# Block 1 of a fused chunk-attention and bilinear-FFN kernel laid out by hand, with the out stores joined in pairs and moved to ScalarE's queue

## The chip, the cores and the metric

The kernel runs on one core of one Trainium2 chip. The metric is the device time of one execution in microseconds (us); below, a time is the median over several executions, with their range. Most executions of one kernel agree within about 1.5%; those more than 1.5% above the fastest of their kernel are labelled slow, and no ratio uses them.

Engine names are those of the profile: PE is TensorE, PEld its weight loads, DVE is VectorE, ACT is ScalarE, POOL is GpSimd, SP is SyncE, and SPq and ACTq are the DMA-issuing instructions of SP and ACT.

## The reference

Attention in chunks of 64 tokens, then a feed-forward layer that multiplies two projections. Inputs and output are fp32.

```python
# q, k, v: (8 batches, 8 heads, 576, 64), cut along the sequence into chunks of 64
scores = (q_c @ k_c^T) / sqrt(64)              # 64x64 in each chunk and head
attn   = exp(scores - max) / (sum + 1e-9)
x      = (attn @ v_c) -> (4608 tokens, 512)    # heads side by side
out    = ((x @ w_a) * (x @ w_b)) @ w_out       # w_a, w_b: 512x1536, w_out: 1536x512
```

## The kernel before

The 4,608 tokens are handled as nine blocks of 512 tokens (K = 0 to 8); a block is two units of 256 (U = 0 to 17). For each unit q, k and v are loaded, cast to bf16 by GpSimd, and q and k are transposed: on TensorE for units 0 to 5, by DMA from unit 6 on (`bring`). The feed-forward layer has six column pairs per block. Block 0 computes them plainly (`ab_step`). From block 1 on, a pair can be done with seven products in place of eight (a Winograd-like scheme, `Group` with `p1` to `p7`), which needs sums of the weights (`combine_w`, four VectorE instructions per pair) and of x. Block 1 does its first two pairs plainly (`PLAIN = 2`). The third product of the kernel, `out_part`, is cut into three parts for each of the four tiles of a block; the third part copies the result to an `o_sb` buffer and stores it.

```python
PE_UNITS = 6
PLAIN = 2
...
    b_pool = ctx.enter_context(tc.tile_pool(name="bsb", bufs=2))
    c_pool = ctx.enter_context(tc.tile_pool(name="csb", bufs=2))
    o_pool = ctx.enter_context(tc.tile_pool(name="osb", bufs=3))
...
    def transpose_dma(U):
        for w, n in ((0, "q"), (1, "k")):
            nc.sync.dma_start_transpose(out=..., in_=raw.pop((n, U))...)   # cut

    def bring(U):
        cast(U, "qk")
        load(U + 1, "q")
        if U < NU:
            transpose_dma(U)
        cast(U, "v")
        load(U + 1, "kv")
...
    def out_part(K, tg, part):
        if part == 0:
            out_ps[K, tg] = bank(psum)
        for ft in range(4 * part, 4 * part + 4):
            nc.tensor.matmul(...)                                           # cut
        if part == 2:
            u, c = divmod(tg, 2)
            o_sb = o_pool.tile([128, DM], FP32, name="o_sb")
            nc.vector.tensor_copy(out=o_sb, in_=out_ps.pop((K, tg)))
            for g in range(2):
                r0 = K * BLK + 256 * u + 128 * g + 64 * c
                nc.sync.dma_start(out=out[r0:r0 + 64, :], in_=o_sb[g * 64:g * 64 + 64, :])
...
        for ft in range(NFT):                     # block 0
            ab_step(0, ft)
            if ft % 2:
                combine_w(ft // 2)
            ...
        cast(4); cast(5); load(6)
        for U in range(PE_UNITS, 8):
            bring(U)
        ...
        for ft in range(2 * PLAIN):               # block 1, the plain pairs
            ab_step(1, ft, 0, 256)
            ...
```

The softmax here doesn't subtract the row's maximum and nothing guards it: scores larger than these inputs give would overflow.

## Time and profile before

| what | value |
|---|---|
| time, 4 executions beside the changed kernel | 332.56 us (330.32 to 334.37) |
| start of block 1, from TensorE's timeline | 47.1 us |
| start of block 2 (first product of its first pair) | 94.5 us |
| from there to the end | 235.6 us, 31.3 us per block on average |
| out stores | 70 on SP's queue, 128 KB each, 2.4 us from issue to landing |

First, the page's slices: the span in 40 equal parts, busy tenths of TensorE, its granted clock in tenths, and the mean busy share of the 16 DMA engines.

```profile
PE   2979784899789999999999999999999999999995
...
PEclk9999799999959999999999999999999999999999
DMA  8999999999989999876978596964111111111223
```

TensorE is full, and at full clock, from the thirteenth slice on. Before that, the DMA engines are full and TensorE and its clock have holes. From slice 29 on (231 us), the loads are over and DMA falls to one tenth: the store traffic that remains is small.

Next, the timeline of TensorE: start, length, line, operation, and in brackets the idle time before it and what ended that.

```profile
51.48 0.60 PE L329 MATMUL ps<-xT,wa 128*128 128x256 f16 x4 [2.05 <-DVE ab_sb L338]
...
58.60 0.61 PE L329 MATMUL ps<-xT,wb 128*128 128x256 f16 x4 [2.80 <-DVE xT L285]
...
92.23 0.63 PE L228 MATMUL ps<-qkt 64*64 64x64 bf16 x30 [3.33 <-DVE o_sb L448]
```

Three holes in block 1: an accumulator bank not yet free, x of unit 3 not yet ready, and an `o_sb` buffer not yet stored. The stage table shows what the last one costs. Its columns are start:end, length, busy us (and instructions) of PE, PEld, DVE, ACT and POOL, granted clock, DMA share, GB/s.

```profile
88.90:92.20 3.30, 0.00 (x0) 0.00 (x0) 0.72 (x2) 0.00 (x0) 1.86 (x2) 0.80 1.02 269
92.20:97.70 5.50, 5.47 (x54) 3.48 (x54) 4.59 (x9) 2.87 (x6) 0.00 (x0) 0.50 0.70 159
97.70:129.00 31.30, 30.43 (x374) 21.37 (x372) 20.10 (x34) 21.28 (x38) 9.37 (x9) 1.00 1.05 218
```

After the hole of 3.3 us TensorE runs 5.5 us at half clock. From 97.7 us on it is full at full clock. In block 2, the DMA engines have no time to spare.

Why the buffer came late is seen in the waits of VectorE (total us, count, longest) and in the timeline of SP's queue (start, length, DMA, count):

```profile
DVE o_sb L448 <- DMA out_dram<-o_sb: 4.0, 1, 4.0
```

```profile
78.13 1.75 SPq L156 DMA_DIRECT2D st<-in_q_dram  x2
80.05 2.84 SPq L210 DMA_TRANSPOSE qkt<-q_raw  x1
82.99 1.25 SPq L210 DMA_TRANSPOSE qkt<-k_raw  x1
...
87.66 5.64 SPq L451 DMA_DIRECT2D out_dram<-o_sb  x8
```

The stores of block 0 are issued at 87.66 us, behind the loads and transposes of units 7 and 8, which stand on the same queue.

### The profile page before, as it was taken

To read this page: it belongs to the slowest core of one execution; us is meant where nothing else is said; L and a number is where in the kernel's file an instruction comes from. 1 tells how busy PE (TensorE), PEld (TensorE's weight loads), DVE (VectorE), ACT (ScalarE), POOL (GpSimd) and SP (SyncE) were. 2 spreads that over 40 slices of the span, in tenths; PEclk is the share of its full clock that TensorE was granted. 3 is DMA by queue.
4 is the path that set the end of the run, shared out by engine and by line. 5 is a ranking of instruction groups with operands and counts; after the bars stand their busy time and mean duration, and the time that the engine had idled before them with its cause. 6 is when DMAs were issued, how large, how long until landed. Compare 5 with 4: busy or idle time off the path is not lost.

```text
span 330.1 us, 7886 instructions
## 1 busy us (share of the span) xinstructions
PE 303.6 (92%) x3222; PEld 205.7 (62%) x3222; DVE 216.7 (66%) x350; ACT 172.2 (52%) x307; POOL 74.6 (23%) x76
## 2 busy tenths in 40 slices
PE   2979784899789999999999999999999999999995
PEld 1534353766556667676777666777776677777743
DVE  3459895746365678587758766857595768666551
ACT  1733355375457655656566566565656464444400
POOL 1566665633213322222121212120000000000000
PEclk9999799999959999999999999999999999999999
DMA  8999999999989999876978596964111111111223
GB/s 238 328 374 284 274 367 230 258 218 246 224 186 236 219 168 233 201 159 162 145 178 179 141 158 163 187 155 110 32 30 38 32 34 34 32 35 43 52 65 96
DMA packets 139331, 53.98 MB, mean 164 GB/s; under 512 B 114592, under 2 KB 133280, under 8 KB 139296
## 3 DMA queue, kind: packets, MB, share of 16 engines
q1 hardware_dynamic: 139136, 53.36, 69.6%
q8 instruction: 25, 0.41, 0.5%
q10 hardware_dynamic: 160, 0.13, 0.2%
q14 instruction: 10, 0.08, 0.1%
HBM read 37.75 MB, written 9.44 MB: 143 GB/s over the span
## 4 chain that ended last, share of the span: by engine, by line
PE 65%; DMA 17%; SPq 8%; DVE 5%; POOL 2%; issue 1%; ACT 1%; ACTq 0%; POOLq 0%; DVEq 0%
PE ps L438 21%; PE pb L375 17%; PE pc L375 11%; PE ps L375 10%; DMA st<-in_moe_w_a_dram 7%; DMA st<-in_q_dram 5%; SPq L156 5%; DMA st<-in_v_dram 4%; PE ps L460 3%; PE ps L243 1%; DVE s L355 1%; SPq L168 1%; SPq L210 1%; PE ps L228 1%; PE ps L276 1%
## 5 line engine op out<-in xcount | busy, mean ns | idle before, releaser
L438 PE MATMUL ps<-wo,ab_sb 128*128 128x512 bf16 x384 | 97.9, 379 | 0.0
L375 PEld LDWEIGHTS <-t 128*128 128x128 f16 x736 | 69.2, 98 | 18.2 <-issue 4.8
L413 DVE TENSOR_TENSOR c_sb<-pc,v_sb 128x512 f32<-128x512 f32 x46 | 31.8, 691 | 55.2 <-ACT v_sb L386 55.2
L375 PE MATMUL pb<-s,t 128*128 128x256 f16 x368 | 56.4, 277 | 0.5 <-ACT u_sb L386 0.5
L375 PE MATMUL ps<-xT,wb 128*128 128x256 f16 x368 | 55.7, 274 | 0.0
L386 ACT COPY u_sb<-pb 128x512 f32<-128x512 f32 x46 | 27.0, 586 | 52.1 <-PE pb L375 52.1
L438 PEld LDWEIGHTS <-ab_sb 128*128 128x128 bf16 x384 | 37.6, 98 | 25.7
L425 DVE TENSOR_TENSOR ab_sb<-pc,c_sb 128x512 bf16<-128x512 f32 x46 | 31.7, 689 | 12.2 <-PE pc L375 11.7
L375 PEld LDWEIGHTS <-wb 128*128 128x128 f16 x368 | 36.3, 99 | 4.5
L425 DVE TENSOR_TENSOR ab_sb<-pb,b_sb 128x512 bf16<-128x512 f32 x46 | 31.5, 685 | 4.4 <-PE pb L375 4.4
L386 ACT COPY v_sb<-pb 128x512 f32<-128x512 f32 x46 | 27.1, 589 | 13.1 <-PE pb L375 12.2
L183 POOL CAST q_raw<-st 128x1024 bf16<-128x1024 f32 x17 | 17.7, 1040 | 71.2 <-DMA st<-in_q_dram 65.6
L414 DVE TENSOR_TENSOR pc<-pc,u_sb 128x512 f32<-128x512 f32 x46 | 31.7, 690 | 0.0
L393 ACT COPY pb<-ps 128x512 f32<-128x512 f32 x46 | 27.3, 594 | 7.7 <-PE ps L375 7.7
L236 ACT ACTIVATE E<-ps 128x512 bf16<-128x512 f32 x34 | 18.6, 594 | 21.8 <-PE ps L228 21.8
L375 PE MATMUL pc<-xT,t 128*128 128x256 f16 x184 | 27.6, 272 | 0.6 <-DVE pc L414 0.5
L375 PE MATMUL pb<-s,wa 128*128 128x256 f16 x184 | 28.1, 276 | 0.0
L375 PE MATMUL pc<-s,t 128*128 128x256 f16 x184 | 28.1, 276 | 0.0
L448 DVE COPY o_sb<-ps 128x512 f32<-128x512 f32 x32 | 21.9, 685 | 9.1 <-PE ps L438 5.0
L183 POOL CAST k_raw<-st 128x1024 bf16<-128x1024 f32 x17 | 17.7, 1040 | 43.8 <-DMA st<-in_k_dram 42.9
L386 ACT COPY b_sb<-ps 128x512 f32<-128x512 f32 x46 | 27.3, 594 | 0.0
L253 ACT ACTIVATE ln<-ps 128x512 f32<-128x512 f32 x34 | 18.6, 595 | 15.6 <-PE ps L243 15.6
(67 smaller groups left out, 312.8 us busy)
## 6 DMA issues: line engine op xcount, KB each, us to landing
out_dram<-o_sb SPq DMA_DIRECT2D x70, 128.0 KB, 2.4
st<-in_v_dram SPq DMA_DIRECT2D x32, 256.0 KB, 4.2
st<-in_q_dram SPq DMA_DIRECT2D x23, 256.0 KB, 4.3
st<-in_k_dram SPq DMA_DIRECT2D x23, 256.0 KB, 3.6
st<-in_moe_w_b_dram SPq DMA_DIRECT2D x6, 512.0 KB, 7.0
st<-in_moe_w_a_dram SPq DMA_DIRECT2D x6, 512.0 KB, 8.0
st<-in_moe_w_out_dram SPq DMA_DIRECT2D x6, 512.0 KB, 7.1
st<-in_q_dram SPq DMA_DIRECT2D x4, 512.0 KB, 5.4
```

The costliest lines, as they stand in the source:

```text
L156: nc.sync.dma_start(out=st[p:p + n, g], in_=src[b, :, s:s + n, :].rearrange("h p d -> p h d"))
L183: eng.tensor_copy(out=raw[n, U], in_=staged.pop((n, U)))
L236: nc.scalar.activation(out=E_of[U][:, j], in_=sc[j], func=AF.Exp, scale=scale)
L253: nc.scalar.activation(out=ln_of[U][:, cl].rearrange("p m n -> p (m n)"), in_=sm[cl], func=AF.Ln)
L375: nc.tensor.matmul(t[:, h * 256:h * 256 + 256], w[:, kt, h * 128:h * 128 + 128], x[:, kt], start=start and h == 0 and kt == 0, stop=h == 1 ...
L386: nc.scalar.copy(out=t, in_=src)
L393: nc.scalar.copy(out=self.B, in_=self.A)
L413: nc.vector.tensor_tensor(out=self.c, in0=self.C, in1=self.v, op=ADD)
L414: nc.vector.tensor_tensor(out=self.C, in0=self.C, in1=self.u, op=ADD)
L425: nc.vector.tensor_tensor(out=self.dst[:, :, c0:c0 + 256], in0=t.rearrange("p (h n) -> p h n", h=2), in1=o.rearrange("p (h n) -> p h n", h=2),
L438: nc.tensor.matmul(out_ps[K, tg], ab_tiles[K][:, ft, tg * 128:tg * 128 + 128], w_out[ft], start=(ft == 0), stop=(ft == NFT - 1),)
L448: nc.vector.tensor_copy(out=o_sb, in_=out_ps.pop((K, tg)))
```

## The change

The intent was to fill the holes of block 1: two more plain pairs, so that weight sums can leave block 0 and be spread in pairs over block 1; unit 3 started first; more buffers for `b_sb`; and the out stores taken off SP's queue, so that they no longer wait behind loads. The core of the diff:

```diff
-PLAIN = 2
+PLAIN = 4
...
-    def combine_w(i):
+    def combine_w(i, part):                      # two of the four sums at a time
...
+            ("wa", (psum_c, psum)[ft % 2] if whole else psum_c),
...
-        b_sb = b_pool.tile([128, BLK], FP32, name="b_sb")
+        b_sb = c_pool.tile([128, BLK], FP32, name=("b_sb", "u_sb", "v_sb", "c_sb")[ft % 4])
...
-            for g in range(2):
-                r0 = K * BLK + 256 * u + 128 * g + 64 * c
-                nc.sync.dma_start(out=out[r0:r0 + 64, :], in_=o_sb[g * 64:g * 64 + 64, :])
+            stores.append((K * BLK + 256 * u, c, o_sb))
+
+    stores = []
+
+    def store():
+        while stores:
+            r0, c, o_sb = stores.pop(0)
+            nc.scalar.dma_start(
+                out=out[r0:r0 + 256, :].rearrange("(g c r) d -> c g r d", g=2, c=2)[c],
+                in_=o_sb,
+            )
...
         for ft in range(NFT):
             ab_step(0, ft)
-            if ft % 2:
-                combine_w(ft // 2)
+            if ft in (9, 10):
+                combo()                          # one half of combine_w
...
         def chunk():
+            store()
             if outs:
                 out_part(*outs.pop(0))
...
+        transpose_pe(3)
         for ft in range(2 * PLAIN):
             ab_step(1, ft, 0, 256)
...
+            if ft >= 5:                          # out parts of block 0 start here
+                chunk()
+                combo()
+        transpose_pe(4)
...                                              # attention of units 4 to 6 re-placed
```

Before, a tile went out as two stores of 64 rows each; now as one store whose DRAM side is 2 x 64 rows of 512.

More of the change, by code (lines that the diff above doesn't have):

```diff
@@ L59 @@
     ab_pool = ctx.enter_context(tc.tile_pool(name="ab", bufs=2))
-    b_pool = ctx.enter_context(tc.tile_pool(name="bsb", bufs=2))
     c_pool = ctx.enter_context(tc.tile_pool(name="csb", bufs=2))
@@ L109 @@
     w_t = {}
-    def combine_w(i):
+    def combine_w(i, part):
         wb, wa = w_ab["wb", i], w_ab["wa", i]
         b11, b12, b21, b22 = wb[:, 0:2], wa[:, 0:2], wb[:, 2:4], wa[:, 2:4]
-        t1, t2, t3, t4 = [
-            wpool.tile([128, 2, WCOL], FP16, name=f"t{j}_{i}") for j in range(1, 5)
-        ]
+        if i not in w_t:
+            w_t[i] = [wpool.tile([128, 2, WCOL], FP16, name=f"t{j}_{i}") for j in range(1, 5)]
+        t1, t2, t3, t4 = w_t[i]
         for o, x0, x1, op in (
-            (t1, b12, b11, SUB),
-            (t3, b22, b12, SUB),
-            (t2, t3, b11, ADD),
-            (t4, b21, t2, SUB),
-        ):
+            ((t1, b12, b11, SUB), (t3, b22, b12, SUB)),
+            ((t2, t3, b11, ADD), (t4, b21, t2, SUB)),
+        )[part]:
             nc.vector.tensor_tensor(out=o, in0=x0, in1=x1, op=op)
-        w_t[i] = (t1, t2, t3, t4)
     def load_wo(i):
@@ L134, in cast_wo @@
         t = wpool.tile([128, 2, DM], BF16, name=f"wo{i}")
-        nc.gpsimd.tensor_copy(out=t, in_=staged.pop(("wo", i)))
+        src = staged.pop(("wo", i))
         for f in range(2):
+            nc.gpsimd.tensor_copy(out=t[:, f], in_=src[:, f])
             w_out[2 * i + f] = t[:, f, :]
@@ L325, in ab_step @@
         ps = {}
-        for n, pool in (("wb", psum_b), ("wa", psum_c)):
-            ps[n] = bank(pool if c1 - c0 == BLK else psum)[:, :c1 - c0]
+        whole = c1 - c0 == BLK
+        for n, pool in (
+            ("wb", psum_b if whole else psum),
+            ("wa", (psum_c, psum)[ft % 2] if whole else psum_c),
+        ):
+            ps[n] = bank(pool)[:, :c1 - c0]
             for kt in range(NKT):
@@ L382, in product, with staged @@
                     )
-        def staged(self, src, name, pool):
-            t = pool.tile([128, 512], FP32, name=name)
+        def staged(self, src, name):
+            t = c_pool.tile([128, 512], FP32, name=name)
             nc.scalar.copy(out=t, in_=src)
@@ L396, in p6 @@
             self.product(self.B, self.t2, self.s2)
-            self.u = self.staged(self.B, "u_sb", c_pool)
+            self.u = self.staged(self.B, "u_sb")
         def p2(self):
             self.product(self.A, self.b21, self.x12)
-            self.b = self.staged(self.A, "b_sb", b_pool)
+            self.b = self.staged(self.A, "b_sb")
         def p5(self):
             self.product(self.B, self.t1, self.s1)
-            self.v = self.staged(self.B, "v_sb", c_pool)
+            self.v = self.staged(self.B, "v_sb")
         def p7(self):
@@ L532, with combo @@
         spread[:] = [psum]
+        combos = [(i, p) for i in range(PLAIN, NWP) for p in range(2)]
+        combos += [(i, p) for i in range(PLAIN) for p in range(2)]
+        def combo():
+            if combos:
+                combine_w(*combos.pop(0))
         for ft in range(NFT):
             ab_step(0, ft)
-            if ft % 2:
-                combine_w(ft // 2)
+            if ft in (9, 10):
+                combo()
             if ft == 6:
@@ L559, in values_x @@
                 combine_x(U // 2)
+        transpose_pe(3)
         for ft in range(2 * PLAIN):
             ab_step(1, ft, 0, 256)
-            if ft == 0:
-                transpose_pe(3)
-            if ft == 2:
+            if ft == 1:
                 scores(3)
-        sums(3)
-        inverse(3)
-        values_x(3)
+                combo()
+            if ft == 3:
+                sums(3)
+                inverse(3)
+        values(3)
+        outs += [(0, tg, p) for tg in range(4) for p in range(3)]
         for ft in range(2 * PLAIN):
             ab_step(1, ft, 256, 512)
-        attention = {
-            (1, PLAIN, 0): [lambda: transpose_pe(4)],
-            (1, PLAIN, 1): [lambda: scores(4)],
-            (1, PLAIN + 1, 0): [lambda: sums(4), lambda: inverse(4), lambda: transpose_pe(5)],
-            (1, PLAIN + 1, 1): [lambda: scores(5)],
-            (1, PLAIN + 2, 0): [lambda: values_x(4)],
-            (1, PLAIN + 2, 1): [lambda: sums(5)],
-            (1, PLAIN + 3, 0): [lambda: inverse(5)],
-            (1, PLAIN + 3, 1): [lambda: values_x(5), lambda: scores(6)],
+            if ft in (1, 2):
+                combo()
+            if ft == 3:
+                combine_x(1)
+            if ft >= 5:
+                chunk()
+                combo()
+        transpose_pe(4)
+        attention = {
+            (1, PLAIN, 0): [chunk, lambda: scores(4)],
+            (1, PLAIN, 1): [chunk, combo, lambda: transpose_pe(5), combo],
+            (1, PLAIN + 1, 0): [lambda: sums(4), lambda: inverse(4), combo],
+            (1, PLAIN + 1, 1): [lambda: scores(5), chunk, lambda: values_x(4)],
             (2, 0, 0): [lambda: sums(6), lambda: inverse(6)],
@@ L614 @@
             for i in range(PLAIN if K == 1 else 0, NWP):
-                if (K, i) in ((1, PLAIN), ) or (K > 1 and i == 1):
+                if K > 1 and i == 1:
                     outs += [(K - 1, tg, p) for tg in range(4) for p in range(3)]
@@ L634 @@
                 chunk()
-                if K == 1:
-                    chunk()
                 attend(K, i, 1)
@@ L640 @@
                 last = now
+            if K == 1:
+                sums(5)
+                inverse(5)
+                chunk()
+                combo()
+                chunk()
+                values_x(5)
+                while outs:
+                    chunk()
+                combo()
+                scores(6)
+                store()
+                assert not combos
         last.add7()
@@ L647 @@
             chunk()
+        store()
         for tg in range(4):
```

## The prediction

> **What bounds the kernel now.** The granted clock is full and TensorE is about 100% busy from 98 us on (slices, stage table), so blocks 2 to 8 run at TensorE's pace and the change can move little there. The loss is before: between the start of block 1 (47.1 us) and the first product of block 2 (94.5 us) the timeline of TensorE shows idle gaps of 2.05, 2.80 and 3.33 us and smaller ones, and after the last of them 5.5 us at a granted clock of 0.50, about 11 us in all. Block 0 loses about 4.7 us more (a 2.1 us wait for a VectorE copy queued behind the weight sums, then half clock). Through 90 us the 16 DMA engines are full (share 1.0 to 1.1). The chain that ended last runs through loads, casts and DMA issues up to 88.5 us, then an out store, then TensorE. The 3.33 us gap is an o_sb buffer waiting for its store (4.0 us), which stood on the SP queue behind the loads of units 7 and 8.
>
> **What the change removes.** 20 of 24 weight sums (0.41 us alone, up to 1.26 us) leave block 0: I estimate block 0 ends 4 us earlier. Two more plain pairs cost 8 matmuls of 0.109 us, 0.9 us. Deeper b_sb and alternating banks remove most gaps of 2 to 3 us in the plain half. If nothing else happened, block 2 would start near 84 us, 10 us earlier.
>
> **What it adds.** Each out store is now an instruction of ScalarE, which stops there until the store's semaphores are reached. The built program shows more than the diff: eight DMA semaphores are handed out in turn, and each DMA waits for the one before it on its semaphore. The first store (block 0, tile 0) waits for unit 7's DMA transpose of q, the second for that of k, the third for the load of v of unit 8. In the trace unit 7's transposes are issued at 80.05 and 82.99 us and land 4.9 and 2.9 us later; they hang on loads, casts and the earlier transposes, none of which the change speeds up. ScalarE reaches the first store near 64 us. So I expect it to stand there until about 85 us. TensorE can go on only until the next out part needs a bank that an E activation of unit 4 has to free, so it idles some 17 to 20 us.
>
> **What remains after 85 us**, by durations in the trace: about 16 us of TensorE work up to the fourth product of block 2, which the kernel before issues at 99.7 us. Add 1.2 us (store, first activation), 2.5 us for 5 us at half clock (the Trainium skill, "TensorE: Matmul & The Clock Gate", What's actually happening, says the clock halves after an idle window of about 3.4 us; this trace agrees: 3.33 us idle, then 5.5 us at 0.50), and 2 to 3 us because ScalarE has to catch up. That gives 106 to 107 us: 6 to 7 us later. The gains of block 0 vanish in the wait. From block 2 on I expect no change; a store costs ScalarE 0.5 to 0.7 us, 4 per 31 us, off the path.
>
> **Prediction:** 340.0 us, 80% range 331.0 to 345.0. Faster by over 2%: 0.10; within 2%: 0.42; slower by over 2%: 0.48.
>
> **What shows it.** Right: ScalarE idle some 20 us before the first E of unit 4, ended by a DMA; TensorE idle there, slices near 0 between 67 and 85 us, half clock after. Wrong: stores issued near 65 us, block 2 starting before 90 us.
>
> **What would make it wrong.** Transposes landing much earlier; a store's wait not holding ScalarE; the 2% line lies at 339.9 us, so a microsecond decides the class.

## More of the kernel before

Finally, the DMA queues, with packets, MB and share of the 16 engines' time:

```profile
q1 hardware_dynamic: 139136, 53.36, 69.6%
...
q10 hardware_dynamic: 160, 0.13, 0.2%
```

q1 is SP's queue, q10 ScalarE's. ScalarE issues only two stores of the last tile here.

## The result, and the profile after

The changed kernel takes **381.27 us** (375.67 to 382.51, four executions) against 332.56 us (330.32 to 334.37) of the kernel before on the same chip. The ratio is 1.138, with a 95% interval of 1.119 to 1.157. It is 13.8% slower, and outside the predicted range of 331 to 345 us. (Each ratio in this document is the mean time of one kernel's fast runs over that of the other's of the same rounds, so not quite the ratio of the medians quoted.) The output is correct.

The profiled execution took 381.4 us.

The page's slices after; a slice is 9.5 us here, 8.25 us before:

```profile
PE   2799877608888792967929778999999999999994
...
PEclk9999999957989997896978969999999999999999
DMA  8999999995799699967899899983110111111114
```

There is one deep hole in slices 8 and 9, as predicted. But TensorE and its clock also show losses in slices 14 to 25, where the kernel before was full. The DMA engines are no less busy there (0.90 to 1.05 of their time from 140 to 233 us, against 0.75 to 0.86 from 129 to 222 us before), yet they move no more: 139 to 164 GB/s against 166 to 168.

**The hole in block 1.** ScalarE's timeline and TensorE's after it:

```profile
69.30 0.65 ACT L394 COPY pb<-ps 128x512 f32<-128x512 f32 x1
84.46 1.16 ACTq L457 DMA_DIRECT2D out_dram<-o_sb  x1
85.66 0.60 ACT L233 ACTIVATE E<-ps 128x512 bf16<-128x512 f32 x1 [15.71 <-issue]
```

```profile
86.31 1.86 PE L439 MATMUL ps<-wo,ab_sb 128*128 128x512 bf16 x4 [13.54 <-ACT E L233]
```

ScalarE ended a copy at 69.9 us, issued its first out store at 84.46 us, and came to E of unit 4 at 85.66 us. (E is the program's tile of exp(scores); it is not the theory E below.) TensorE stood 13.5 us for it. Block 2 starts at 101.7 us, 7.2 us later than before. This is close to what was predicted (about 85 us, and 6 to 7 us later).

**The loss after that.** From the start of block 2 to the end the kernel takes 277.8 us, against 235.6 before: 42.2 us more, where no change was predicted. TensorE's timeline has a hole like these in several blocks:

```profile
149.90 1.01 PE L376 MATMUL pb<-s,wa 128*128 128x256 f16 x4 [7.49 <-ACT v_sb L387]
...
173.21 1.01 PE L376 MATMUL pb<-s,wa 128*128 128x256 f16 x4 [5.51 <-ACT v_sb L387]
...
198.32 1.01 PE L376 MATMUL pb<-s,wa 128*128 128x256 f16 x4 [7.02 <-ACT v_sb L387]
```

TensorE waits for ScalarE's copy `v_sb`. What did ScalarE wait for? Its waits (total, count, longest):

```profile
ACT ln L259 <- DMA st<-in_v_dram: 16.8, 2, 8.7
...
ACT ln L259 <- DMA qkt<-q_raw: 6.7, 1, 6.7
...
ACT E L233 <- DMA qkt<-k_raw: 5.2, 1, 5.2
```

No ln and no E reads these DMAs' data: `ln` at L259 reads the ln tile itself, and E the bank of scores. The store just ahead of them in ScalarE's order is what waits, and the profile counts its wait to the next computing instruction. ScalarE's timeline before the first of TensorE's holes above shows it, down to the copy that TensorE waits for:

```profile
147.75 0.52 ACTq L457 DMA_DIRECT2D out_dram<-o_sb  x1
148.32 1.06 ACT L259 ACTIVATE ln<-ln 128x1024 f32<-128x1024 f32 x1 [8.65 <-DMA st<-in_v_dram]
149.28 0.57 ACT L387 COPY v_sb<-pb 128x512 f32<-128x512 f32 x1
```

What the store waits for is a load of v, or a transpose, that lands late. So why are loads late? SP's queue:

```profile
80.69 1.64 SPq L207 DMA_TRANSPOSE qkt<-q_raw  x1
82.43 1.25 SPq L207 DMA_TRANSPOSE qkt<-k_raw  x1
...
87.20 10.54 SPq L153 DMA_DIRECT2D st<-in_q_dram  x2
...
104.47 6.81 SPq L153 DMA_DIRECT2D st<-in_k_dram  x2
```

The transposes of unit 7 are where they were (80.69 us, before 80.05). But two loads of q now take 10.54 us to issue and two of k 6.81 us; two loads of q took 1.75 us before. Between busy stretches, the DMA engines look idle at times. The following is a window of the DMA view, 84 to 100 us in 40 slices of 0.4 us, busy tenths and GB/s:

```profile
DMA  9914999999968863111111111159921211115992
GB/s 259 204 30 101 244 276 298 261 256 226 247 155 201 204 175 90 50 46 52 51 46 47 52 47 52 46 150 282 281 76 52 66 52 46 52 52 145 276 273 57
```

In the long stretch of ones, loads are outstanding, yet only between one and two tenths of the 16 engines' time is busy and 46 to 52 GB/s are moved. Two full engines of sixteen would print just that (0.125). The trace does not name the engine of a packet, so that it is two engines is for the experiments and the packet counts to show. The stage table (same columns as before) and the queues:

```profile
90.00:110.00 20.00, 16.91 (x256) 10.71 (x257) 15.94 (x29) 14.07 (x25) 3.22 (x3) 0.91 0.77 90
```

```profile
q1 hardware_dynamic: 134016, 44.97, 63.3%
q10 hardware_dynamic: 4320, 8.52, 6.7%
```

From 90 to 110 us only 90 GB/s are moved, against 218 GB/s in the first full stage before. Queue q10 carries the stores now: 8.52 MB in 4,320 packets.

### The profile page after: what moved, and what is told of

Same layout as the page of the kernel before. It is cut to its first block, busy times and chain, and to the rows that moved or that the text cites. A ratio compares the mean times of both kernels' runs of the same rounds, so it can differ in the third digit from the quotient of the medians.

```text
span 379.5 us, 7825 instructions
## 1 busy us (share of the span) xinstructions
PE 310.0 (82%) x3185; PEld 210.4 (55%) x3230; DVE 209.4 (55%) x350; ACT 170.6 (45%) x307; POOL 74.6 (20%) x82
## 3 DMA queue, kind: packets, MB, share of 16 engines
q10 hardware_dynamic: 4320, 8.52, 6.7%
## 4 chain that ended last, share of the span: by engine, by line
PE 33%; DMA 31%; SPq 28%; POOL 3%; issue 2%; ACTq 0%; ACT 0%; DVEq 0%; DVE 0%; POOLq 0%
SPq L153 21%; DMA st<-in_q_dram 12%; PE ps L439 11%; PE pb L376 9%; DMA st<-in_v_dram 8%; DMA st<-in_moe_w_a_dram 6%; PE pc L376 6%; PE ps L376 6%; SPq L207 5%; DMA st<-in_k_dram 3%; DMA out_dram<-o_sb 3%; POOL v_raw L180 2%; POOL q_raw L180 1%; SPq L165 1%; PE ps L273 1%
## 5 line engine op out<-in xcount | busy, mean ns | idle before, releaser
L439 PE MATMUL ps<-wo,ab_sb 128*128 128x512 bf16 x342 | 93.7, 384 | 16.7 <-ACT E L233 13.5
L414 DVE TENSOR_TENSOR c_sb<-pc,v_sb 128x512 f32<-128x512 f32 x44 | 30.4, 691 | 90.5 <-ACT v_sb L387 90.0
L376 PEld LDWEIGHTS <-t 128*128 128x128 f16 x704 | 67.7, 100 | 22.7 <-issue 8.0
L376 PE MATMUL pb<-s,t 128*128 128x256 f16 x352 | 55.3, 281 | 3.1 <-ACT u_sb L387 3.0
L387 ACT COPY u_sb<-pb 128x512 f32<-128x512 f32 x44 | 25.7, 585 | 57.6 <-PE pb L376 47.2
L376 PEld LDWEIGHTS <-wa 128*128 128x128 f16 x176 | 17.6, 100 | 39.5 <-issue 28.5
L376 PEld LDWEIGHTS <-wb 128*128 128x128 f16 x352 | 35.5, 101 | 5.1
L426 DVE TENSOR_TENSOR ab_sb<-pc,c_sb 128x512 bf16<-128x512 f32 x44 | 30.3, 689 | 12.4 <-PE pc L376 12.0
L233 ACT ACTIVATE E<-ps 128x512 bf16<-128x512 f32 x34 | 18.6, 595 | 37.4 <-issue 15.7
L180 POOL CAST v_raw<-st 128x1024 bf16<-128x1024 f32 x18 | 18.7, 1041 | 73.1 <-DMA st<-in_v_dram 37.4
L259 ACT ACTIVATE ln<-ln 128x1024 f32<-128x1024 f32 (+1 forms) x19 | 19.2, 1013 | 28.6 <-DMA st<-in_v_dram 16.8
L426 DVE TENSOR_TENSOR ab_sb<-pb,b_sb 128x512 bf16<-128x512 f32 x44 | 30.1, 684 | 3.6 <-PE pb L376 3.6
L415 DVE TENSOR_TENSOR pc<-pc,u_sb 128x512 f32<-128x512 f32 x44 | 30.3, 689 | 0.0
```

Source lines behind the costliest of these rows:

```text
L180: eng.tensor_copy(out=raw[n, U], in_=staged.pop((n, U)))
L233: nc.scalar.activation(out=E_of[U][:, j], in_=sc[j], func=AF.Exp, scale=scale)
L259: nc.scalar.activation(out=rs_of[U][:, c], in_=ln_of[U][:, c], func=AF.Exp, scale=-1.0)
L376: nc.tensor.matmul(t[:, h * 256:h * 256 + 256], w[:, kt, h * 128:h * 128 + 128], x[:, kt], start=start and h == 0 and kt == 0, stop=h == 1 ...
L387: nc.scalar.copy(out=t, in_=src)
L414: nc.vector.tensor_tensor(out=self.c, in0=self.C, in1=self.v, op=ADD)
```

## The experiments

Names: `a_` is built from the changed kernel, `b_` from the kernel before. `sp`, `act` and `pool` name the queue that issues the out stores. `2` means one store of 2 x 64 rows for a tile, `16` two stores of 64 rows. "Block 2" is the start of the first product of block 2, "rest" the span from there on.

Two theories. **W**, the predicted one: the stores on ScalarE's queue wait for other DMAs, and ScalarE stands. **E**, its rival for the larger loss: the single 2 x 64-row store is carried by only two of the 16 DMA engines. E comes from the Trainium skill, "DMA: Bandwidth & Descriptors", section "Why a DMA increments its semaphore by 16 and not by 1": the hardware looks at the outermost dimension of each side and "picks the largest k ≤ 16 that divides both of those dim sizes". The new store has 2 on the DRAM side and 128 on the SBUF side, which gives 2; a store of 64 rows has 64 on both, which gives 16.

| kernel | median us | ratio [95%] | block 2 at | rest |
|---|---|---|---|---|
| before | 332.56 | 1 | 94.5 | 235.6 |
| changed (= act, 2) | 381.27 | 1.138 [1.119, 1.157] | 101.7 | 277.8 |
| a_act16 | 340.63 | 1.025 [1.017, 1.033] | | |
| a_act16_again | 340.71 | 1.026 [1.019, 1.032] | 102.9 | 236.5 |
| a_sp2 | 365.64 | 1.098 [1.090, 1.105] | 97.7 | 263.4 |
| a_sp16 | 330.11 | 0.994 [0.986, 1.002] | 92.3 | 236.0 |
| a_pool (16) | 327.98 | 0.977 [0.969, 0.986] | 92.1 | 236.9 |
| a_act16_b7 | 331.14 | 0.997 [0.991, 1.003] | 94.4 | 235.9 |
| a_act16_b67 | 329.29 | 0.993 [0.986, 0.999] | 85.8 | 241.8 |
| a_sp16_c4 | 325.29 | 0.978 [0.969, 0.987] | 86.2 | 237.2 |
| a_pool_c4 | 323.85 | 0.975 [0.971, 0.979] | 86.3 | 236.5 |
| b_c4 | 328.62 | 0.990 [0.984, 0.995] | 90.5 | 235.5 |
| b_sp2 | 366.94 | 1.106 [1.099, 1.113] | 102.1 | 266.0 |
| b_act16 | 384.36 | 1.155 [1.146, 1.163] | | |
| b_act16_later | 346.38 | 1.040 [1.033, 1.046] | 108.2 | 236.7 |
| a_act2_b67 | 383.82 | 1.152 [1.146, 1.159] | 99.5 | 279.5 |

Ratios are to the kernel before in the same rounds (its medians were 332.2 to 333.8 us). For a_act16 the median is that of its three fast executions; the other medians are of all executions, and in the changed kernel, a_pool and a_sp16_c4 these include some slow. "Block 2" and "rest" are those of the profiled execution, which is one of these in the changed kernel and in a_pool. All kernels gave correct results.

### Only the shape undone: a_act16

```diff
-            nc.scalar.dma_start(
-                out=out[r0:r0 + 256, :].rearrange("(g c r) d -> c g r d", g=2, c=2)[c], in_=o_sb)
+            for g in range(2):
+                r = r0 + 128 * g + 64 * c
+                nc.scalar.dma_start(out=out[r:r + 64, :], in_=o_sb[g * 64:g * 64 + 64, :])
```

> The changed kernel with each out store written as two DMAs of 64 rows, still issued by ScalarE. Theory W (the store's wait for an earlier DMA on its semaphore holds ScalarE) alone: still near 381 us, as nothing about the waits is taken away. Theory E (a store whose outermost size is 2 runs on 2 of the 16 DMA engines, takes some 6 us and holds up the loads) alone: 322 to 332 us. Both, W for block 1 and E for the stalls of blocks 2 to 5: 336 to 344 us, ScalarE still standing from about 70 to 84 us, no stall over 3 us after 130 us.

Its three fast executions took 340.04, 340.63 and 342.54 us. A fourth took 449.84 us at a granted clock of 0.663 from beginning to end; it was the profiled one, so nothing is read from its trace, and no cause for that clock was found. The kernel was run again for a profile:

> a_act16 once more, since its profile fell in an execution at a granted clock of 0.66. Expected: 340 to 343 us, ScalarE standing from about 70 to 84 us before the first E of unit 4, block 2 starting near 101 us, no wait of TensorE over 3 us after 110 us.

It took 340.71 us with block 2 at 102.9 us and the rest 236.5 us, as before the change. So with the shape undone no loss is left after the start of block 2, and the queue alone holds block 2 back by some 10 us (it starts at 92.3 us in a_sp16 below). The packets of its SP and ScalarE queues, the latter to compare with 4,320 in the changed kernel:

```profile
q1 hardware_dynamic: 134016, 44.97, 55.3%
q10 hardware_dynamic: 5280, 8.52, 9.9%
```

The same 8.52 MB take 960 packets more. They fit the engine counts: 128 rows as two stores on 16 engines are 2 x (64 + 16) = 160 packets, if each engine adds one at the end, which is what the skill says of the semaphore in the section cited. One store on two engines is 128 + 2 = 130. For the 32 tiles, the difference is 32 x 30 = 960, exactly.

The packed trace, counted packet by packet, agrees. Packets of 4 bytes, the size of a semaphore write, number two for each of the changed kernel's 32 tile stores and 16 for each of the 64 stores here. And the stores' packets of 2 KB never overlap more than fourfold in the changed kernel (one or two are under way for 95% of the time in which any is), but up to 19 at once here.

### Only the queue undone: a_sp2

```diff
-            nc.scalar.dma_start(
+            nc.sync.dma_start(
                 out=out[r0:r0 + 256, :].rearrange("(g c r) d -> c g r d", g=2, c=2)[c],
```

> The changed kernel with the same single store of 2x64 rows, issued by the SP queue in place of ScalarE. W: ScalarE no longer stands, so 325 to 333 us. E: loads still late in blocks 2 to 5, so 355 to 380 us, with SP issues of loads taking 3 to 7 us and DMA slices near 50 GB/s, but no 14 us gap of ScalarE at 70 us.

It took 365.64 us, as E expected. Without any store on ScalarE, 263.4 us remain from block 2 on, 27 more than with the two-store form. SP's queue and one of TensorE's waits:

```profile
88.08 9.74 SPq L457 DMA_DIRECT2D out_dram<-o_sb  x4
97.88 10.64 SPq L153 DMA_DIRECT2D st<-in_q_dram  x2
```

```profile
236.52 0.64 PE L225 MATMUL ps<-qkt 64*64 64x64 bf16 x32 [4.33 <-DMA qkt<-k_raw]
```

Four such stores take 9.74 us on SP's queue, and two loads of q behind them 10.64 us. TensorE then waits for a transpose that came late. The shape also costs something in block 1: block 2 starts at 97.7 us, 5.4 us later than in a_sp16 below, after a hole of 9.10 us for an `o_sb` buffer. A rival, that SP's loads only stand in semaphore waits for the slow stores, is not seen: in the waits of SP's queue no load and no transpose waits for a store, here or in the changed kernel.

### Both undone: a_sp16, and stores from GpSimd: a_pool

```diff
-                nc.scalar.dma_start(out=out[r:r + 64, :], ...)     # of a_act16
+                nc.sync.dma_start(out=out[r:r + 64, :], ...)       # a_sp16
+                nc.gpsimd.dma_start(out=out[r:r + 64, :], ...)     # a_pool
```

> The changed kernel with both undone: stores as two DMAs of 64 rows on the SP queue. This is the rest of the change alone. Both theories: no ScalarE gap at 70 us, no late loads. Stores stand behind the loads of units 7 and 8 in the SP queue as before, so the fourth o_sb copy waits until about 91 us and block 2 starts at 93 to 96 us: 327 to 334 us.

> The changed kernel with stores as two DMAs of 64 rows issued by GpSimd, whose DMAs have semaphores of their own in the build, so no store waits for a load. W and E: no ScalarE gap; stores of block 0 leave once GpSimd has cast v of unit 7 (about 82 us), block 2 starts at 86 to 92 us: 322 to 331 us.

They took 330.11 and 327.98 us. So the change without its store edit gains 0.6% (not told apart from no change), and with GpSimd's queue 2.3%, from two fast executions (325.0 and 325.4 us; the other two, 330.6 and 330.8, are slow), so whether it is over 2% is unclear. In the build, GpSimd's stores also have semaphores of their own; a_pool does not tell that apart from GpSimd having time to spare. With a_sp16 as the base, the queue costs 340.7 - 330.1 = 10.6 us, the shape 365.6 - 330.1 = 35.5 us, and both together 381.3 - 330.1 = 51.2 us. In a_sp16 there was a hole of its own:

```profile
91.72 0.64 PE L225 MATMUL ps<-qkt 64*64 64x64 bf16 x30 [6.85 <-DVE o_sb L449]
```

The old wait for `o_sb` (3.33 us before) is now 6.85 us. The out parts come earlier, but their stores still stand behind the loads of units 7 and 8, and there are three buffers. This is where the gain of the layout had gone.

### The wait alone moved: a_act16_b7 and a_act16_b67

In the program as built, eight semaphores are handed to the DMAs of SP and ScalarE in turn, and each DMA waits for the one before it on its semaphore. The order in which the program names the DMAs thus decides what a store waits for. These two kernels move only the place of a `bring`; in the first, every engine still has the same instructions in the same order (compared in the built programs), and only the waits differ.

```diff
-        for U in range(PE_UNITS, 8):
-            bring(U)
+        bring(6)                       # a_act16_b7; a_act16_b67 has neither here
...
                 store()
+                bring(7)               # a_act16_b67: bring(6); bring(7), ahead of scores(6)
                 assert not combos
```

> As a_act16 (two stores of 64 rows each, on ScalarE), with the line that brings unit 7 moved in the program behind the stores of block 0. The build keeps the order of instructions of every engine; only the semaphores change hands: the first store now waits for the transposes of unit 6 (landed about 76 us) in place of those of unit 7 (about 85 us), the second for k and v of unit 7 (about 81 us). W: ScalarE is released at about 76 us, 333 to 338 us. If the wait for the semaphore is not what holds ScalarE: 340 to 343 us as a_act16.

> The same with units 6 and 7 both brought behind the stores of block 0 in the program; every engine's order stays (but for two E activations of ScalarE, which come one place earlier). The first store now waits for loads of units 4 and 5, landed before it is reached. W: no gap of ScalarE near 70 us, block 2 starts at 84 to 89 us, 322 to 329 us, so the layout by hand gains what it was meant to. If W is wrong: 340 us.

They took 331.14 and 329.29 us, the first slightly better than expected, the second just above the expected 322 to 329. ScalarE's timeline of a_act16_b7:

```profile
76.30 1.35 ACTq L459 DMA_DIRECT2D out_dram<-o_sb  x2
77.70 1.08 ACT L233 ACTIVATE E<-ps 128x512 bf16<-128x512 f32 x2 [8.03 <-DMA qkt<-k_raw]
```

and of a_act16_b67:

```profile
67.50 0.56 ACTq L459 DMA_DIRECT2D out_dram<-o_sb  x1
...
70.18 1.09 ACT L233 ACTIVATE E<-ps 128x512 bf16<-128x512 f32 x2 [1.36 <-PE ps L225]
```

The stores are released at 76.3 and 67.5 us in place of 83.8 in a_act16_again. Since the first of these kernels differs from a_act16 in waits alone, W is shown: the store does hold ScalarE until another DMA, of no concern to it, has landed. In a_act16_b67 block 2 starts at 85.8 us, 17 us earlier than in a_act16. But the rest is longer, 241.8 us. There the wait has only changed sides: on the same eight semaphores, loads on SP's queue now wait for stores. From the waits of SP's queue, and TensorE's timeline:

```profile
SPq L153 <- DMA out_dram<-o_sb: 16.4, 7, 3.4
```

```profile
105.34 0.49 PE L225 MATMUL ps<-qkt 64*64 64x64 bf16 x32 [3.11 <-DMA qkt<-k_raw]
```

### A fourth buffer: a_sp16_c4, b_c4 and a_pool_c4

```diff
-            o_sb = o_pool.tile([128, DM], FP32, name="o_sb")
+            if (K, tg) == (0, 3):
+                o_sb = c_pool.tile([128, DM], FP32, name="c_sb")
+            else:
+                o_sb = o_pool.tile([128, DM], FP32, name="o_sb")
```

> As a_sp16 (stores as in the kernel before), with the fourth out tile of block 0 copied into a c_sb buffer, so that no copy of block 0 waits for a store. If the 6.85 us gap of TensorE at 85 us in a_sp16 is that wait, it goes, with the half clock behind it: 321 to 326 us. If the loads of unit 8 end the wait in truth, the time stays at 327 to 331 us and the gap is put down to a transpose.

> The kernel before, with only that one buffer changed. If its 3.33 us gap and the 5.5 us of half clock behind it are that wait: 326 to 330 us. If the loads bound it: 331 to 334 us.

> a_pool with the fourth out tile of block 0 in a c_sb buffer, as in a_sp16_c4. The 5 us gap of TensorE at 86 us goes, with half clock after it: 320 to 325 us, level with or a little under a_sp16_c4.

All three hit: 325.29, 328.62 and 323.85 us. The last tile of block 0 takes a buffer that is free in that stage, and the hole is gone. The kernel before gains 1.0% by this alone; the layout by hand then is worth 3.3 us more (328.6 to 325.3). a_pool_c4 is the best of all, 2.5% faster than the kernel before: hand layout, two stores of 64 rows on GpSimd's queue, and the fourth buffer. (Six `o_sb` do not fit.)

### Each cause on the kernel before: b_sp2, b_act16, b_act16_later

```diff
             for g in range(2):          # b_sp2
-                r0 = K * BLK + 256 * u + 128 * g + 64 * c
-                nc.sync.dma_start(out=out[r0:r0 + 64, :], in_=o_sb[g * 64:g * 64 + 64, :])
+            r0 = K * BLK + 256 * u
+            nc.sync.dma_start(
+                out=out[r0:r0 + 256, :].rearrange("(g c r) d -> c g r d", g=2, c=2)[c], in_=o_sb)
...
-                nc.sync.dma_start(...)  # b_act16: at once behind the copy;
+                nc.scalar.dma_start(...)  # b_act16_later: at the start of the next chunk
```

> The kernel before, with its two stores of 64 rows joined into the one store of 2x64 rows of the change, still on the SP queue. E alone: each store's 128 rows of 2 KB go through 2 engines at some 90 ns each, about 6 us, and the loads share these engines; TensorE waits for transposes in blocks 2 to 6: 358 to 372 us. If the slow stores hurt only where ScalarE issues them: 331 to 337 us.

> The kernel before, with its stores of 64 rows issued by ScalarE in place of SP. W alone, on the old layout: in the build the first store waits for the transposes of unit 7 (about 86 us), the second for k and v of unit 8 (about 91 us), the third for a transpose of unit 8, so ScalarE stands from about 70 us: 339 to 350 us. If W needs the new layout: 329 to 334 us.

> b_act16 with each store issued one out part after its copy, as in the change. If the place behind the copy cost the 37.6 us per block of b_act16 (31.3 us in the kernel before): blocks 3 to 8 back at 31 to 32 us each, 340 to 352 us in all. If the waits for loads cost it: 370 to 390 us.

b_sp2 took 366.94 us, as E expected: the shape alone, on the kernel before, costs some 35 us. Its SP queue has

```profile
q1 hardware_dynamic: 138176, 53.36, 62.1%
```

which is 960 packets less than before the change (139,136), again the number of E.

b_act16 missed: 384.36 us where 339 to 350 was expected. I had taken it that only the first stores would wait. TensorE's timeline shows a wait in every block:

```profile
177.07 0.60 PE L375 MATMUL pb<-s,wa 128*128 128x256 f16 x4 [1.76 <-ACT v_sb L386]
...
214.70 0.60 PE L375 MATMUL pb<-s,wa 128*128 128x256 f16 x4 [1.74 <-ACT v_sb L386]
```

The wait itself is short (1.7 us), but the block takes 37.6 us (214.70 - 177.07) in place of 31.9 (from 160.90 to 192.75 us for the same products in the kernel before). The store stands right behind its own VectorE copy, so ScalarE waits for that copy four times a block, and what it owes TensorE comes late. The changed kernel issues a store one chunk later. With that delay, b_act16_later took 346.38 us and its rest is 236.7 us, as before; this one hit. So the rule "a store costs ScalarE its issue time" holds only when what the store waits for is long done.

### The wait removed while the shape stays: a_act2_b67

```diff
     # the moves of a_act16_b67, applied to the changed kernel, its single 2 x 64 store kept
```

> The changed kernel with its single store of 2x64 rows on ScalarE, and units 6 and 7 brought behind the stores of block 0 in the program, so that the first store waits for loads landed long before. E: no gap of ScalarE near 70 us, but the loads late in blocks 2 to 5 and ScalarE standing in stores that wait for them: 358 to 376 us. If the late loads came from the wait in block 1: 325 to 340 us.

It took 383.82 us, above the expected range, and no less than the changed kernel. With the slow shape, moving the wait gains nothing: SP's loads now stand for stores (13.0 us in all, 10.1 at the longest), and block 2 starts at 99.5 us, since TensorE waits for unit 6's transposes instead,

```profile
98.90 0.65 PE L225 MATMUL ps<-qkt 64*64 64x64 bf16 x32 [11.04 <-DMA qkt<-k_raw]
```

and the rest is 279.5 us. So the two causes are not independent. The costs of 10.6 and 35.5 us are each measured with the other absent. How the 277.8 us of the changed kernel's rest divide between slow loads and ScalarE's waits for those late loads is not settled: no run removes all of ScalarE's waits while keeping both the shape and the queue. That a_sp2's rest is 263.4 us says that some 14 us of it need the stores on ScalarE.

## Why the prediction was right and wrong

**Right: the wait in block 1.** The prediction had ScalarE reach its first store near 64 us and stand until about 85; it stood from 69.9 to 84.5. It expected TensorE idle for 17 to 20 us; it was 13.5. It expected block 2 to start 6 to 7 us later; it was 7.2 us. The idle times were put too long because ScalarE came to the store later than expected; this cost the forecast little, as it counted from the store's release, and that was right (84.5 us). a_act16, which has this part alone, takes 340.6 to 340.7 us: the predicted 340.0 is the time of that kernel. a_act16_b7 shows the mechanism.

**Right in kind: half clock after a long hole.** The Trainium skill, "TensorE: Matmul & The Clock Gate", section "What's actually happening", gives an idle window of about 3.4 us; the kernel before shows 3.33 us idle, then 5.5 us at a granted clock of 0.50. The prediction took 5 us for the changed kernel; after its hole of 13.5 us, 2.9 us ran at half clock (86.3 to 89.2 us), and 6.0 us in a_act16_again. The length of a hole alone does not settle it in these traces: before, the clock fell 2.0 us into the hole of 3.33 us (at 90.9 us), a hole of 2.11 us (to 36.25 us) was followed by 3.4 us at half clock, and one of 2.80 us (to 58.60 us) by none.

**Right: the gains of block 0 vanish in the wait.** Block 1 does start earlier, at 44.3 us (43.8 in a_sp16) against 47.1, some 3 us where 4 were estimated, but TensorE meets the wait all the same. What the prediction didn't see is that even without that wait most of the gain would be lost to the `o_sb` buffers (a_sp16, a hole of 6.85 us), and needs the fourth buffer to appear.

**Wrong: "From block 2 on I expect no change; a store costs ScalarE 0.5 to 0.7 us, 4 per 31 us, off the path."** This is the step that failed, and it was mis-sized by 42.2 us. I took the time to issue a store for its cost, and did not ask what the DMA itself would do in its new shape. What the runs show in its place: the new store is carried by two engines of 16. From the queue's share, its packets take 6.7% x 16 x 379.5 us / 4,320 = 94 ns each. So one store (130 packets, 65 on each of two engines) takes about 6.1 us on them, an estimate; spread over 16 engines (160 packets at 102 ns in a_act16_again) it would be about 1.0 us on each. Four such stores are some 24 us of each 31-us block on these two engines. They already have their share of the loads: SP's queue in a_act16_again, which carries the loads without the 64 tile stores, took 55.3% of 339.4 us, over nine blocks about 21 us per block and engine. That is some 45 us of work for 31 us (an estimate from means). A load is spread over all 16 engines and ends when its last share has landed, and the share beside the stores is the last. (The trace does not name the engine of a packet; this step is inferred from the packet counts, the slow issues and the stretches of one tenth. The loads' packets fit it: of those of 256 bytes between 100 and 233 us, 6.6% take more than 60 ns, against 0.4% in a_act16_again.) So loads, transposes and everything that waits for them come late, and ScalarE's stores wait for those loads in turn. The loss stops when the loads do: from 260 us to 300 us TensorE is busy again for 39.6 of 40 us, though the stores go on.

The profile before contained the warning: full DMA engines beside a full TensorE in block 2, and at least three quarters full until 222 us. There, doubling the work of two of them could not be free. The rule that gives two engines stands in the skill, in a section that the prediction didn't look up, for it counted the edit of the stores as a change of queue alone.

**The class.** The chances put 0.48 on slower by over 2%, which came, but mostly by the cause that was not foreseen: the wait in block 1 alone gives 1.026, which is not clear of 2%. The range assumed that only the wait in block 1 could cost, so its upper end of 345 us left no room for a second cause.

## What to carry to other kernels

When a diff rewrites a DMA's access pattern, look at the outermost dimension on both sides before anything else: merging two stores into one can take a DMA from 16 engines down to two, and when the engines are already full, every load behind it gets slower. A store issued from a computing engine makes that engine stand in all of the store's waits, including those that the build adds for semaphores taken in turn; check in the built program what it waits for, and give it to an engine that has nothing to do. When one removed wait gains nothing, look for the next resource that was hidden behind it: here a buffer that one spare tile supplied.

## What the Trainium skill lacked or had wrong

- "DMA: Bandwidth & Descriptors", section "Issuing engines are not separate DMA queues", says that starting DMAs from several engines only saves the sequencer's time to start them. The runs show a cost that it leaves out: the issuing engine also stands in the DMA's waits. (That semaphore waits happen on the issuing sequencer is said elsewhere on the page, without a cost.) ScalarE was idle for 15.7 us ahead of one E activation, and moving the stores to it cost 10.6 us (a_sp16 to a_act16_again); moving the same stores to GpSimd cost nothing (327.98 us against 330.11).
- The same page has the rule for the number of engines, and the packet counts agree with it exactly (960 packets of difference, changed to a_act16_again and before to b_sp2). It gives no cost for stores on few engines beside loads on all. Here 4 stores of 256 KB per 31-us block on two engines, beside loads on all 16, cost 35.5 us of 330; the DMA view then shows, in stretches, one tenth busy and 46 to 52 GB/s, which looks like idle engines.
- No page that I read tells that semaphores taken in turn tie DMAs of different queues to each other. Two kernels with the same instruction order on every engine, differing in these waits alone, took 340.63 and 331.14 us.
- "TensorE: Matmul & The Clock Gate" has no case like the one execution of a_act16 at a granted clock of 0.663 throughout (449.84 us against 340.63). The cause stays open.
